# A DeltaNet layer with a multiplicative feed-forward: the second inverse in PSUM, weight signs by a GpSimd product, and another order of steps

## The chip, the cores and the metric

The kernel runs on one core of a Trainium2 chip. A core has five engines with queues of their own, which run in parallel and wait for one another by semaphores: TensorE (PE, matrix products, results in PSUM), VectorE (DVE), ScalarE (ACT), GpSimd (POOL) and SyncE (SP, which here issues most DMA transfers). The metric is the time of one execution on the device in microseconds; lower is better. The profile's span, from the first to the last instruction, is some microseconds shorter than the timed execution.

## The reference

```python
# attention: q, k, v of (B, H, S, D) = (4, 8, 768, 48), beta of (4, 8, 768)
k_n = k / (norm(k, axis=-1) + 1e-6)
for t in range(S):
    y[t] = q[t] @ state
    v_old = k_n[t] @ state
    state = state + beta[t] * outer(k_n[t], v[t] - v_old)
# feed-forward on x = y as (3072 tokens, 384 features)
a = x @ w1                # (384, 1024)
b = x @ w2                # (384, 1024)
h = a * b @ w3            # (1024, 1024)
out = h @ w_out           # (1024, 384)
```

The inputs are single precision, but for the four weight matrices, which come as doubles: each weight is two 32-bit words.

## The kernel before

**Attention.** The 768 tokens are cut into 12 chunks of 64 (index m or c), and two chunks make a unit j or u. Within a chunk the recurrence is a triangular system: the kernel computes the scores of keys with keys and queries with keys (`scores`, step `s`), inverts the unit lower triangular matrix, and applies it. The inverse is done for 32x32 blocks: the blocks of two chunks are written to DRAM and read back so that each of the 128 partitions has one whole block (`to_blocks`, step `u`; tile `Ub`). `inverse` (step `V`) then eliminates in 31 steps on VectorE, each a product into `tb` and a subtraction from the matrix V. Before the change V of unit 0 lies in PSUM (it takes one of the two buffers `ps_w` from `two_banks()` and keeps it, marked in `held`, until it is copied back to `Vb`), and V of the other five units lies in SBUF. The result goes through DRAM once more into `TT`, and `corner` (step `e`: a VectorE transpose L421, two rounds of TensorE products, two pairs of ScalarE copies) makes the 64x64 inverse from its blocks. `chain` (step `c`) carries the state from chunk to chunk, `outputs` (step `y`) makes y and, for the second chunk of a unit, issues the transfers that complete the tile `xT` (L601).

**Feed-forward.** The product w3 w_out is folded into one matrix `w34` of 1024x384: `transpose_w3` (step `t`) turns pieces of w3, `fold` (step `f`, two halves) multiplies them by w_out (`wo`). `wo` lies in the memory of `w2s`, so w2's pieces can be written only where the folds have read it. Then for each unit `ab` (step `a`, eight per unit: product with w1, ScalarE copy, product with w2, VectorE product) and `o` (step `o`, four per unit). These two steps are most of TensorE's work.

**Weights.** `piece` (step `P`) turns doubles into singles in four steps: the transfer into one of five buffers `raw` (shared with the tile `a` of `ab`), two ScalarE activations (absolute value of the high word, scaled; the low word, scaled), a shift left by 3 and an instruction that sets the sign bit from the high word on VectorE (L625, L626), and an integer addition of the low part on GpSimd (L630). P0 to P7 are w_out, P8 to P23 w3 (P of 8 + n belongs to t of n), P24 to P29 w1 and P30 to P35 w2, the first three of each for `a` steps 0 to 3.

**The order.** Each step is a generator; the string ORDER, written out, names the steps one by one, and a name's nth place is its nth stretch up to a `yield`. The program text, and with it the order of instructions in each engine's queue, follows ORDER exactly (`in_text_order`). Letters not told above: `k`, `q`, `v` load, `p` loads the permuted k and q that `d` transposes on VectorE, `K` and `Q` do the same by TensorE for the first two chunks, `g` squares and sums, `N` norms, `n` scales v by norms.

Of the kernel before, what the change touches and what calls it, by code (L numbers as in the profile page):

```python
# [51 lines left out]
v3 a01 a01 a01 a00 a00 a00 P29 P29 a02 P29 P29 a02 c1 a03 a03 a04 k5 g2 d4 V1 e2 g2 g2 c2 n3
n3 e2 e2 e2 a07 d4 d4 P35 P35 e2 e2 d4 e3 e3 P33 a05 n2 n2 c2 g2 s4 N2 e3 s4 s4 s4 P34 P34
c2 P35 P34 e3 e3 s4 P33 P33 P33 a07 a04 s4 a06 c2 y2 p5 d5 d5 u4 c2 P34 y2 P35 a04 p5 d5 d5
c2 a05 a05 a05 v4 n4 s5 s5 s5 c3 c3 a04 a06 a06 a06 V2 s5 s5 u5 s5 e3 c3 a07 k6 c3 y3 V2 a07
o03 o03 V2 V2 V2 y3 V2 V2 V2 V2 V2 V2 V2 V2 V2 o00 V2 p6 p6 g3 y3 n4 V2 V2 V2 V2 V2 o03 V2
V2 V2 v5 V2 V2 V2 V2 V2 V2 o01 o01 o01 o00 o02 a13 a13 o02 a14 a14 V2 V2 V2 V2 V2 e4 e4 g3
a12 a15 a15 o02 d6 d6 a12 a12 a12 a10 a10 e5 e4 c3 a14 e5 e4 c3 n5 c4 e4 e4 c4 a13 a13 a14
e5 k7 g3 g3 g3 V3 c4 a16 a16 c4 c4 c4 y4 y4 d6 v6 d6 g3 g3 a17 s6 g3 N3 s6 s6 s6 s6 s6 n5
a17 a17 p7 d7 d7 p7 d7 o00 d7 a16 c5 c5 e5 k8 e5 e5 a17 a15 s7 s7 a15 s7 s7 s7 s7 u6 u7 a16  # L60
a11 c5 a10 c5 a11 a11 v7 y5 y5 n6 a10 a11 o10 g4 o13 o13 V3 V3 V3 g4 o10 V3 V3 V3 V3 V3 V3
V3 V3 V3 y5 a25 a25 p8 p8 o10 a23 a23 o13 V3 V3 V3 V3 V3 V3 V3 V3 V3 V3 V3 V3 o12 o12 V3 V3
V3 V3 V3 V3 V3 V3 V3 e6 g4 e6 a26 a26 o11 o11 o11 a26 e7 a25 c5 e7 c5 g4 e6 a23 k9 a23 e6
a25 n6 a26 g4 g4 c6 g4 e6 e6 a21 c6 c6 d8 d8 d8 d8 a21 g4 c6 a24 a24 y6 N4 c6 c6 y6 a24 s8
s8 s8 s8 p9 p9 d9 d9 p10 a22 e7 s8 s8 a24 d9 d9 a21 s9 s9 e7 s9 s9 V4 a22 a22 s9 a21 c7 n7
n7 c7 s9 u8 u9 V4 V4 V4 a22 V4 V4 V4 e7 e7 a27 c7 o12 k10 v8 n8 a20 a20 V4 V4 c7 a20 a27 a27
y7 y7 c7 a27 v9 a20 o21 o23 y7 a36 o21 o21 o23 o23 V4 V4 V4 g5 g5 V4 V4 V4 o20 V4 V4 o20 d10
a36 V4 V4 V4 V4 c7 a36 V4 V4 V4 V4 V4 n8 V4 V4 V4 V4 V4 a35 a35 k11 p10 V4 V4 V4 g5 a36 e8
e8 a34 a34 g5 g5 g5 a35 a30 a30 e8 a35 c8 c8 a31 v10 e8 e8 d10 d10 d10 g5 g5 s10 N5 s10 n10
s10 o22 o22 e9 e9 a31 a34 a34 e8 c8 e9 a30 e9 e9 c8 c8 a37 a37 y8 c8 c9 a30 n9 n9 o22 c9 y8  # L70
p11 a37 d11 s10 p11 e9 d11 a33 a33 d11 d11 s10 s10 s11 s11 s11 s11 s11 s11 u10 u11 a32 a32
a37 a31 a31 a32 c9 c9 a32 V5 V5 V5 V5 V5 a33 c9 y9 y9 y9 V5 a33 o20 V5 V5 o33 o33 o33 V5 V5
V5 o31 o31 o31 V5 V5 V5 V5 V5 V5 V5 c9 a43 a43 a43 V5 V5 V5 a43 v11 a40 a40 V5 V5 V5 V5 V5
V5 a47 a47 V5 V5 V5 V5 V5 V5 a42 a42 o32 o30 o30 a44 c10 a44 o32 n11 V5 e10 e10 e10 a42 a42
a41 n11 a41 a47 n10 a47 c10 e10 e10 o32 a40 e10 c10 e11 e11 e11 c10 a40 a44 a44 c10 y10 c10
a41 a41 e11 e11 y10 c11 c11 a46 e11 c11 a45 a45 a45 a45 a46 a46 c11 a46 y11 o30 y11 y11 o40
o40 o40 o42 o42 o42 a53 a53 a53 a53 a50 a52 a50 a52 a51 a51 a51 o41 o41 o43 o43 o43 a51 a50
a50 a55 a55 a55 a55 a56 o41 a56 a56 a56 a57 a52 a52 a57 a57 a57 a54 a54 a54 a54 o51 o51 o51
o50 o50 o50 o52 o52 o53 o53 o53 o52
# [4 lines left out]
def kernel(  # L84
# [286 lines left out]
    def inverse(j):  # L371
        Vb = in_turn(work, [P, BS, BS], "Vb", 1, "Vb")
        pool.memset(Vb[:], 0.0)
        pool.memset(Vb[:].rearrange("p s t -> p (s t)")[:, 0 : BS * BS : BS + 1], 1.0)
# [12 lines left out]
        for s in range(BS - 1):
            n = BS - 1 - s
            t = in_turn(work, [P, 256], "tb", 2, "tb")
            tv = t[:, 0 : (s + 1) * n].rearrange("p (r t) -> p r t", t=n)  # L390
            dve.tensor_tensor(  # L391
                out=tv, in0=V[:, 0 : s + 1, s : s + 1].to_broadcast([P, s + 1, n]),
                in1=U[:, s, s + 1 : BS].unsqueeze(1).to_broadcast([P, s + 1, n]), op=ALU.mult,
            )
# [1 line left out]
            dve.tensor_tensor(out=o, in0=o, in1=tv, op=ALU.subtract)  # L396
# [213 lines left out]
    def piece(n, srcs, dst):  # L610

        raw = in_turn(ffn, [P, CW, 2], "raw", 5, "raw", U32)
        for rows, src in srcs:
# [12 lines left out]
        dve.scalar_tensor_tensor(  # L626
            out=du, in0=hi, scalar=0x80000000, in1=du, op0=ALU.bitwise_and, op1=ALU.bitwise_or
        )
        yield
        pool.tensor_tensor(out=du, in0=du, in1=lo, op=ALU.add)  # L630
# [207 lines left out]
```

## Time and profile before

| | |
|---|---|
| time, median of 3 | 628.66 us (627.59 to 628.71) |
| span of the profiled execution | 623.6 us |
| PE busy | 580.3 us (93%) |
| DVE busy | 352.2 us (56%) |
| ACT busy | 161.1 us (26%) |
| POOL busy | 102.1 us (16%) |
| first product of a step `a` (L694) | at 139.44 us |
| last TensorE instruction ends | at 619.7 us |

Busy shares are means over a kernel of two halves: up to 139 us weights are converted and folded while the first unit goes through attention, and from there on the feed-forward of one unit runs beside the attention of the next. They have to be read by stretches. In a table of groups, the columns are line, engine, operation, output and inputs with their shapes and count, then busy time in us and the mean of one in ns, then the idle time of the engine in front of them and what ended it. In a list by time, the columns are start and length in us, engine, line, operation. Instructions of one engine overlap a little at their ends, so the distance of two starts can be shorter than the first one's length.

### The profile page before, as it was taken

Reading aid. Unit: us, or ns where it says so; the run is one execution under the profiler, and the core shown is the slowest. Engines: PE = TensorE matmul, PEld = TensorE weight load, DVE = VectorE, ACT = ScalarE, POOL = GpSimd, SP = SyncE. Lnnn points to the kernel's source line nnn. Section 1 sums busy time; section 2 is a strip of 40 time slices with the busy share of each in tenths; the row PEclk is TensorE's granted clock in tenths of the full one; section 3 lists DMA queues with packets and bytes.
Section 4 is the critical chain, followed back from the end, with each engine's and each line's share of the span. In section 5 each row is a group of like instructions: output and inputs, shape, how many; then the busy total and the mean of one; then the engine's idle time right before and its main releaser. Section 6 shows DMA issues by size and latency. Waiting matters only on the chain.

```text
span 623.6 us, 17022 instructions
## 1 busy us (share of the span) xinstructions
PE 580.3 (93%) x7372; PEld 343.1 (55%) x7372; DVE 352.2 (56%) x764; ACT 161.1 (26%) x333; POOL 102.1 (16%) x114
## 2 busy tenths in 40 slices
PE   3838779979999999999999999999999999999997
PEld 2724457744575655665556655466564556545454
DVE  3599879999856674667827659464397032100100
ACT  3573236642241112311113111123011022210100
POOL 5364453402321100201002010120001000000000
PEclk9857888999999999999999999999999999999999
DMA  9678966886742724443444453333311200000001
GB/s 207 163 211 169 239 153 140 195 150 107 174 65 52 126 76 87 64 77 80 70 106 52 68 120 73 68 67 43 69 40 39 72 23 3 26 14 25 0 14 38
DMA packets 201835, 55.60 MB, mean 89 GB/s; under 512 B 191969, under 2 KB 195041, under 8 KB 201761
## 3 DMA queue, kind: packets, MB, share of 16 engines
q1 hardware_dynamic: 197600, 53.74, 41.7%
q10 hardware_dynamic: 4160, 0.79, 0.8%
q8 instruction: 58, 0.95, 0.7%
q14 instruction: 17, 0.13, 0.1%
HBM read 42.30 MB, written 11.01 MB: 85 GB/s over the span
## 4 chain that ended last, share of the span: by engine, by line
PE 81%; DMA 7%; SPq 4%; DVE 3%; issue 2%; ACT 2%; POOL 1%; DVEq 0%; ACTq 0%; POOLq 0%
PE ps_f L694 41%; PE ps_f L714 20%; PE ps_w L474 6%; PE ps_w L569 4%; PE ps_w L322 3%; DMA raw<-in_moe_w_dram 3%; SPq L212 2%; PE ps_t L444 2%; PE ps_t L430 2%; PE ps_f L674 2%; DMA vtok<-in_v_dram 1%; DMA ktok<-in_k_dram 1%; DMA X<-in_q_dram 1%; DMA raw<-in_moe_w_out_dram 1%; SPq L614 1%
## 5 line engine op out<-in xcount | busy, mean ns | idle before, releaser
L694 PE MATMUL ps_f<-xT,w1s 128*128 128x512 f32 x288 | 132.9, 605 | 4.3 <-DMA xT<-xT 4.3
L694 PE MATMUL ps_f<-xT,w2s 128*128 128x512 f32 x288 | 131.7, 599 | 0.0
L714 PE MATMUL ps_f<-w,ab 128*128 128x384 f32 x384 | 126.4, 488 | 0.0
L714 PEld LDWEIGHTS ps_f<-w,ab 128*128 128x128 f32 x384 | 72.5, 190 | 51.1 <-issue 3.0
L708 DVE TENSOR_TENSOR ab<-a,ps_f 128x512 f32<-128x512 f32 x48 | 32.5, 683 | 112.7 <-PE ps_f L694 112.6
L694 PEld LDWEIGHTS ps_f<-xT,w1s 128*128 128x128 f32 x288 | 53.9, 192 | 66.0 <-issue 63.2
L694 PEld LDWEIGHTS ps_f<-xT,w2s 128*128 128x128 f32 x288 | 53.1, 190 | 60.3 <-issue 56.8
L703 ACT COPY a<-ps_f 128x512 f32<-128x512 f32 x48 | 27.5, 586 | 142.6 <-PE ps_f L694 132.9
L391 DVE TENSOR_TENSOR tb<-Vb,Ub 128x31 f32<-128x31 f32 (+15 forms) x155 | 55.5, 358 | 13.0 <-DMA Ub<-Ud 8.2
L396 DVE TENSOR_TENSOR Vb<-Vb,tb 128x31 f32<-128x31 f32 (+15 forms) x155 | 58.4, 377 | 5.3
L674 PE MATMUL ps_f<-w2s,w3T 128*128 128x384 f32 x128 | 50.0, 550 | 3.6 <-POOL w2s L630 2.1
L234 POOL TENSOR_TENSOR sq<-ktok 128x384 f32<-128x384 f32 x24 | 20.7, 862 | 152.0 <-DVE ss L236 91.6
L590 ACT COPY xT<-ps_w 48x256 f32<-48x256 f32 x96 | 30.4, 365 | 54.2 <-PE ps_w L569 53.7
L720 ACT COPY osb<-ps_f 128x384 f32<-128x384 f32 x24 | 11.3, 479 | 127.4 <-PE ps_f L714 109.1
L460 POOL TENSOR_TENSOR vtok<-vtok,n 128x384 f32<-128x384 f32 x24 | 19.9, 842 | 130.6 <-DMA vtok<-in_v_dram 104.3
L674 PEld LDWEIGHTS ps_f<-w2s,w3T 128*128 128x128 f32 x128 | 26.8, 215 | 23.3 <-issue 6.9
L322 PE MATMUL ps_w<-KQ 48*64 48x128 f32 x768 | 30.5, 303 | 5.3 <-DVE KQ L285 2.7
L322 PEld LDWEIGHTS ps_w<-KQ 48*64 48x64 f32 x768 | 25.0, 150 | 13.9 <-issue 5.5
L665 PE MATMUL ps_f<-ident,w 128*128 128x128 f32 x64 | 13.4, 363 | 13.5 <-POOL w L630 13.5
L630 POOL TENSOR_TENSOR w<-w,raw 128x512 uint32<-128x512 uint32 x16 | 21.2, 1332 | 26.6 <-ACT w L622 7.8
L534 DVE TENSOR_TENSOR S<-S,ps_w 48x768 f32<-48x768 f32 x20 | 19.0, 949 | 11.0 <-PE ps_w L474 10.7
L331 DVE TENSOR_TENSOR U<-ps_w,wt 128x512 f32<-128x512 f32 x24 | 16.4, 686 | 15.0 <-PE ps_w L322 14.6
(83 smaller groups left out, 558.3 us busy)
## 6 DMA issues: line engine op xcount, KB each, us to landing
raw<-in_moe_w_dram SPq DMA_DIRECT2D x16, 512.0 KB, 6.2
vtok<-in_v_dram SPq DMA_DIRECT2D x24, 192.0 KB, 4.0
raw<-in_moe_w_dram SPq DMA_DIRECT2D x24, 192.0 KB, 4.0
out_dram<-osb SPq DMA_DIRECT2D x24, 192.0 KB, 2.0
ktok<-in_k_dram SPq DMA_DIRECT2D x22, 192.0 KB, 4.3
raw<-in_moe_w_out_dram SPq DMA_DIRECT2D x8, 384.0 KB, 3.8
Ud<-U SPq DMA_DIRECT2D x48, 64.0 KB, 2.0
Ub<-Ud SPq DMA_DIRECT2D x6, 512.0 KB, 4.6
```

The costliest lines, as they stand in the source:

```text
L322: pe.matmul(ps[half(z), h % 2, 128 * (h // 2) : 128 * (h // 2) + 128], lhsT=x[:, 0, :], rhs=x.rearrange("p j t -> p (j t)"), start=True, s ...
L391: dve.tensor_tensor(out=tv, in0=V[:, 0 : s + 1, s : s + 1].to_broadcast([P, s + 1, n]), in1=U[:, s, s + 1 : BS].unsqueeze(1).to_broadcast( ...
L396: dve.tensor_tensor(out=o, in0=o, in1=tv, op=ALU.subtract)
L474: pe.matmul(out(ps, r, h, z), lhsT=lhs(r, h, z), rhs=rhs(r, h, z), start=True, stop=True,)
L569: i = pe.matmul(region(h, z, r), lhsT=lhs, rhs=rhs, start=part[n] not in part[:n], stop=part[n] not in part[n + 1 :],)
L590: act.copy(out=xT[f, p:NP:2, b : b + NR, cc, :].rearrange("p a r t -> p r a t"), in_=pyv[f, z, b : b + NR],)
L630: pool.tensor_tensor(out=du, in0=du, in1=lo, op=ALU.add)
L674: pe.matmul(ps[:, 0:DM], lhsT=w3Ts[jc, kc // 4][:, kc % 4 * P : kc % 4 * P + P], rhs=wo[:, kc], start=(kc == 0), stop=(kc == KF - 1),)
L694: pe.matmul(ps[:], lhsT=w[:, m, js], rhs=x[:, m].rearrange("p b c t -> p (b c t)"), start=(m == 0), stop=(m == KM - 1),)
L703: act.copy(out=a[:], in_=ps[:])
L708: dve.tensor_tensor(out=t[:], in0=a[:], in1=ps[:], op=ALU.mult)
L714: pe.matmul(ps[:, 0:DM], lhsT=abs_[u, jc][:, b * P : (b + 1) * P], rhs=w34[:, jc, :], start=(jc == 0), stop=(jc == KF - 1),)
```

## The change

Three things are changed.

- `inverse` keeps V in PSUM for units 0 and 1 instead of unit 0 alone. For unit 1 this adds two ScalarE copies in front and two behind, and holds one `ps_w` buffer in between.
- `piece` no longer sets the sign bit on VectorE. ScalarE turns the high word into +1 or -1 (Sign, in place, a third activation), and GpSimd multiplies the absolute value by it, after its integer addition. This is to take work from VectorE.
- ORDER is a new one, with the same steps but for the four copies of V1. At its start V0's memset and P11's load come first, and q0's load stands behind P11's activations in ScalarE's queue. The first `a` stands at place 367 in both.

Of the orders only the part up to the first `a` is shown here, beside the rest of the diff.

```diff
-P3 P6 k0 g0 q0 P3 P3 P3 g0 g0 k1 K0 K0 P6 P6 K0 K0 K0 Q0 Q0 Q0 Q0 Q0 g0 g0 g0 g0 K1 K1 K1 K1
-K1 g0 beta beta beta N0 P15 s0 s0 s0 q1 s0 s0 s0 s0 Q1 Q1 Q1 Q1 Q1 P6 P15 P15 P15 s1 s1 s1
-P11 s1 s1 P11 s1 P11 P13 P13 p2 d2 P11 t3 d2 V0 P14 P14 P14 P10 P10 P13 u0 u1 P12 P0 P10 V0
-V0 s1 V0 P12 P12 P0 P0 V0 P13 P14 V0 P10 V0 V0 V0 P2 P2 P2 t5 P12 t5 V0 V0 P0 t4 t3 P1 P1 P1
-V0 V0 V0 P1 t4 t7 t7 P2 P5 P5 P5 t2 P4 V0 t6 t6 P7 f3 P7 P7 P7 p3 k2 t2 f1 V0 V0 P22 P23 f2
-P4 P4 V0 p2 V0 P22 P22 V0 P23 P23 P4 P5 f1 f3 f2 g1 f3 s0 V0 V0 V0 V0 V0 V0 V0 V0 P21 P8 P8
-V0 V0 V0 V0 V0 f2 P23 t15 t15 v0 n0 f1 P22 P9 t14 n0 t14 f7 V0 k3 V0 P16 V0 V0 f7 P17 g1 f7
-P8 g1 g1 P9 P9 V0 d2 P8 t0 P21 d2 s2 P21 g1 g1 P9 e0 t1 P16 P16 t0 P21 t13 e0 e0 g1 t1 g1 N1
-s2 s2 e1 s2 P16 t8 v1 n1 s2 s2 e0 e0 e0 s1 f0 e1 c0 P26 t8 P26 t13 e1 n1 d3 P17 P20 P20 P19
-P19 P17 P17 f0 e1 c0 y0 y0 c0 P26 P20 f0 e1 P19 P20 t12 p3 d3 t12 d3 d3 c0 s3 s3 t9 s3 s3
-P26 P27 P27 s3 P19 t11 s3 c1 c1 u2 P28 P28 P28 e1 f6 P27 k4 V1 g2 g2 c1 P18 P18 P18 t11 c1
-P28 P24 P24 t9 P24 u3 P25 f6 y1 V1 V1 V1 V1 P27 P25 P25 V1 V1 f6 V1 c1 V1 V1 y1 V1 V1 V1 V1
-P18 t10 t10 g2 p4 V1 V1 V1 V1 V1 f4 V1 P31 f5 P31 P30 P30 P30 V1 f4 v2 P32 f4 f5 P32 P32 y1
-P24 P25 a02 P31 a02 V1 V1 V1 V1 V1 V1 V1 p4 V1 V1 f5 a03 g2 V1 V1 V1 a03 P30 P32 a00 P31 a01
...
+V0 P11 k0 g0 k1 g0 g0 P11 P11 P1 P11 q0 K0 K0 K0 K0 K0 P3 K1 g0 g0 P1 P1 P1 K1 K1 K1 K1 g0
+g0 P3 P3 Q0 P14 Q0 Q0 Q0 P3 Q0 beta beta t3 g0 P14 beta q1 Q1 Q1 Q1 N0 p2 Q1 Q1 s0 P14 P14
+s0 s0 s0 s0 s0 s0 P0 P0 s1 s1 s1 s1 s1 P12 P12 s1 P0 P0 P12 P12 P15 P15 P15 P15 P13 P13 P13
+P13 u0 u1 P10 V0 V0 t3 P10 d2 d2 V0 P10 V0 V0 V0 V0 V0 V0 P10 v0 n0 P2 P2 P2 P2 t4 t4 t7 V0
+V0 V0 P6 P6 P6 P6 V0 V0 t7 t5 t5 P5 P5 P5 P5 t2 t2 V0 V0 P4 P4 P4 V0 V0 s1 p2 P7 P7 P4 P22
+P7 P7 V0 V0 t6 t6 f2 s0 P22 P22 V0 V0 p3 V0 V0 V0 P9 P9 P9 P23 P23 P16 P22 f1 f1 f2 V0 V0
+P23 f1 V0 f2 n0 t14 t14 P21 P21 P8 P8 V0 V0 P9 V0 V0 V0 V0 P23 k2 g1 g1 f3 f3 V0 V0 k3 g1 P8
+P8 g1 g1 P21 t15 P16 P16 t15 f3 P18 P18 f7 f7 V0 f7 d2 d2 s2 P16 t8 P17 P17 t0 t1 d3 d3 t8
+g1 g1 e0 e1 e0 e0 t1 g1 N1 P18 s2 s2 t0 e0 s2 s2 P19 s2 P21 t13 t13 P17 e0 v1 f0 e0 c0 V1
+P18 t10 P19 c0 y0 y0 e1 e1 e1 p3 d3 d3 P17 s3 t9 s3 s3 P25 s3 s1 s3 s3 P20 P20 P19 P19 c0
+P25 P20 f0 f0 P25 P24 n1 n1 P26 e1 P24 e1 u2 u3 V1 V1 V1 P27 t10 p4 t9 P20 c0 c1 f4 c1 c1
+P27 V1 P24 V1 V1 V1 V1 V1 t12 t12 f4 f4 f6 P24 V1 V1 v3 c1 V1 P26 y1 y1 P25 P27 P27 t11 t11
+P30 V1 V1 V1 P26 V1 P26 k4 g2 P31 v2 n2 f5 P30 f6 f6 V1 V1 V1 V1 P30 V1 c1 f5 f5 P30 V1 V1
+V1 P31 P31 y1 a03 a02 V1 V1 P31 P32 P32 P32 P32 a02 V1 V1 V1 V1 V1 V1 V1 V1 a03 k5 P29 P29
+P29 P29 g2 d4 d4 a00 a02 a03 p4 a00 a00 V1 V1 P28 P28 V1 a02 a01 g2 g2 g2 c1 c2 P28 g2 n2
...
@@ -377,7 +377,7 @@
         sync.dma_start(out=U[:], in_=Uds.pop(j)[:])
         yield
         V = Vb
-        if j == 0:
+        if j < 2:
 
             V = two_banks().rearrange("p a (s t) -> p (a s) t", t=BS)
             held.add(("w", turns["w"]))
@@ -395,7 +395,7 @@
             o = V[:, 0 : s + 1, s + 1 : BS]
             dve.tensor_tensor(out=o, in0=o, in1=tv, op=ALU.subtract)
             yield
-        if j == 0:
+        if j < 2:
             for i in range(0, BS, BS // 2):
                 act.copy(out=Vb[:, i : i + BS // 2], in_=V[:, i : i + BS // 2])
                 yield
@@ -621,13 +621,12 @@
 
         act.activation(out=dst, in_=hi.bitcast(FP32), func=ACTF.Abs, scale=2.0**-112)
         act.activation(out=lo, in_=lo, func=ACTF.Copy, scale=2.0**-29)
+        act.activation(out=hi.bitcast(FP32), in_=hi.bitcast(FP32), func=ACTF.Sign)
         yield
         dve.tensor_scalar(out=du, in0=du, scalar1=3, scalar2=None, op0=ALU.logical_shift_left)
-        dve.scalar_tensor_tensor(
-            out=du, in0=hi, scalar=0x80000000, in1=du, op0=ALU.bitwise_and, op1=ALU.bitwise_or
-        )
         yield
         pool.tensor_tensor(out=du, in0=du, in1=lo, op=ALU.add)
+        pool.tensor_tensor(out=dst, in0=dst, in1=hi.bitcast(FP32), op=ALU.mult)
         yield
 
     w1s = const.tile([P, KM, DF], FP32, name="w1s")
```

More of the change, by code (lines that the diff above doesn't have):

```diff
@@ L50 @@
-P18 t10 t10 g2 p4 V1 V1 V1 V1 V1 f4 V1 P31 f5 P31 P30 P30 P30 V1 f4 v2 P32 f4 f5 P32 P32 y1
-P24 P25 a02 P31 a02 V1 V1 V1 V1 V1 V1 V1 p4 V1 V1 f5 a03 g2 V1 V1 V1 a03 P30 P32 a00 P31 a01
[L52 to L79, printed above, removed]
+V0 P11 k0 g0 k1 g0 g0 P11 P11 P1 P11 q0 K0 K0 K0 K0 K0 P3 K1 g0 g0 P1 P1 P1 K1 K1 K1 K1 g0
@@ new lines @@
+V1 P31 P31 y1 a03 a02 V1 V1 P31 P32 P32 P32 P32 a02 V1 V1 V1 V1 V1 V1 V1 V1 a03 k5 P29 P29
+P29 P29 g2 d4 d4 a00 a02 a03 p4 a00 a00 V1 V1 P28 P28 V1 a02 a01 g2 g2 g2 c1 c2 P28 g2 n2
+a03 e2 e2 e2 g2 P33 e2 P33 a00 d4 d4 a01 a01 e3 P34 P34 c2 e2 e2 g2 N2 s4 s4 s4 P34 a01 P28
+a04 s4 n3 s4 c2 P33 P33 s4 a05 a05 c2 c2 P35 P35 p5 P35 P35 P34 y2 a07 e3 e3 c2 p5 y2 a04 d5
+d5 p6 d5 d5 u4 s5 s5 s5 s5 s5 a06 e3 e3 c3 n3 c3 s5 a06 u5 V2 V2 V2 V2 V2 V2 V2 a06 a06 e3
+c3 V2 a07 a07 a05 a04 c3 y3 y3 y3 a07 a05 a04 o02 o02 o01 V2 V2 V2 V2 V2 V2 V2 V2 o02 V2 V2
@@ new lines @@
+V2 a15 a15 a15 V2 o01 V2 V2 V2 a14 v4 n4 V2 V2 V2 V2 V2 V2 V2 V2 V2 V2 V2 o03 o03 a15 d6 d6
+o00 V3 e4 e5 e4 c3 c3 e4 o01 a14 o00 a14 a14 k6 g3 g3 g3 e4 e4 e5 e4 c4 n4 c4 a12 a12 e5 e5
+g3 p7 k7 c4 v5 c4 o00 p6 d6 d6 g3 e5 a12 c4 a17 y4 y4 a12 n5 c4 c5 n5 v6 c5 a17 g3 g3 g3 N3
+a13 d7 d7 o03 a10 a10 a10 p7 a10 d7 d7 a13 s6 s6 s6 k8 p8 e5 s6 s6 u6 s6 a17 a17 s7 s7 s7 s7
+s7 a11 a11 g4 u7 s7 a11 a11 V3 V3 V3 p8 a13 a13 c5 c5 g4 a16 a16 a16 v7 V3 c5 a16 o12 o12 c5
+c6 o12 y5 y5 y5 o10 o10 o10 o11 o11 V3 V3 V3 n7 V3 V3 V3 V3 V3 a27 a27 a27 n6 n6 V3 c6 V3 V3
@@ new lines @@
+V3 V3 V3 V3 V3 V3 V3 a21 V3 V3 d8 d8 d8 o11 d8 a27 V3 V3 V3 V3 V3 V3 V3 V3 V3 k9 e6 s8 a21
+a25 o13 o13 e6 a26 o13 a25 a26 a26 e6 g4 g4 g4 g4 g4 a24 g4 N4 s8 s8 e7 e7 s8 e6 e6 e6 s8 s8
+a21 a21 a26 e7 c6 c6 a24 a24 a24 p9 p9 c6 c6 y6 y6 d9 a23 d9 d9 p10 d9 a20 s9 a20 s9 s9 a23
+s9 s9 n7 a25 a25 c7 c7 k10 g5 V4 u8 u9 V4 s9 e7 e7 g5 V4 V4 V4 V4 V4 a22 e7 c7 c7 V4 V4 V4
+V4 a22 a22 g5 a23 a20 a20 a22 V4 y7 y7 c7 a23 o22 o22 d10 d10 p11 o23 V4 o23 V4 V4 V4 y7 a36
+V4 V4 V4 V4 V4 c7 g5 a32 a32 v8 V4 V4 V4 V4 V4 a35 a36 a35 V4 V4 V4 V4 V4 V4 V4 p10 a31 a31
@@ new lines @@
+a32 o21 a32 V4 e8 n8 e8 o22 e9 e9 n8 o23 c8 e8 e8 k11 a37 a37 e8 o20 e8 c8 c8 c8 o21 a33 a33
+a33 d10 d10 c8 c8 a33 g5 o20 o20 y8 g5 y8 g5 a35 a35 a30 e9 e9 g5 N5 v9 n9 c9 n9 c9 a36 a36
+s10 e9 s10 s10 s10 p11 s10 e9 a34 a34 v10 d11 d11 d11 d11 c9 c9 a30 s10 a34 s11 o21 s11 s11
+s11 s11 s11 a37 a37 a34 u10 a31 a31 a30 a30 V5 u11 V5 V5 V5 y9 y9 y9 V5 V5 V5 V5 V5 V5 V5 c9
+o31 o31 o30 a41 o30 o30 o31 V5 V5 V5 V5 V5 V5 V5 V5 V5 V5 n10 a44 a44 a41 a42 a42 a45 a45
+a41 V5 V5 V5 V5 a44 v11 V5 V5 V5 V5 V5 V5 V5 V5 n10 o33 V5 a41 c9 o32 o32 e10 e10 e10 o33
@@ L80 @@
+o33 o32 c10 a44 e11 a42 a42 e10 e11 e10 a46 e10 c10 c10 c10 e11 a46 a46 n11 a46 c10 a47 c10
+a40 a40 a40 a47 a47 a47 c11 n11 c11 e11 e11 e11 a43 a40 a43 a43 a43 y10 y10 c11 a45 c11 y11
+a45 o41 o43 y11 y11 o41 o41 o43 o43 a54 a56 a56 a54 a54 a53 a53 a54 a53 a53 o42 o42 a52 o40
+o40 o40 a50 a52 a56 a50 a50 a56 a50 a55 a55 a55 a55 a57 a57 a57 a57 a51 a52 a52 a51 a51 o42
+a51 o50 o50 o50 o51 o51 o51 o53 o53 o53 o52 o52 o52
 """
```

## The prediction

> **What bounds the kernel now.** I first cut the execution into stretches and read the busy columns of each (TensorE, weight loads, VectorE, ScalarE, GpSimd, then the granted clock).
>
> ```profile
> core 0: us, PE busy (x) PEld busy (x) DVE busy (x) ACT busy (x) POOL busy (x), PEclk, DMA share, GB/s
> 0.00:31.00 31.00, 18.07 (x396) 15.90 (x396) 13.11 (x34) 13.54 (x24) 13.57 (x23) 0.93 0.88 186
> 31.00:51.00 20.00, 6.67 (x26) 5.00 (x26) 18.89 (x36) 13.68 (x28) 10.98 (x10) 0.59 0.76 199
> 51.00:89.30 38.30, 31.05 (x114) 18.31 (x114) 31.08 (x71) 13.76 (x26) 17.80 (x18) 0.83 0.80 186
> 89.30:139.40 50.10, 45.32 (x948) 32.17 (x948) 46.04 (x90) 27.63 (x57) 18.64 (x17) 0.93 0.82 168
> 139.40:619.70 480.30, 479.18 (x5888) 271.72 (x5888) 243.06 (x538) 92.00 (x201) 41.07 (x49) 1.00 0.32 62
> ```
>
> From 139.4 us on TensorE never pauses (479.2 of 480.3 us), and its work is untouched. All that can change is when this starts. Ahead of it TensorE idles 38 us and runs partly at a granted clock of 0.59 to 0.93, VectorE is full (18.9 of 20 us, later 46 of 50), and GpSimd and ScalarE are half idle. So the question is the first `a` product, which stands at place 367 of either order, behind the same folds, scores and chains.
>
> Next the chain that ended last. It goes through weight pieces on VectorE at 38 to 44 us, then, at the end of the first stretch, through this:
>
> ```profile
> 135.39 0.59 SPq L601
> ...
> 136.71 2.60 DMA xT<-xT
> 139.44 25.04 PE ps_f L694 x54
> ```
>
> The folds were done at 135.1; TensorE waited 4.3 us for the transfer of xT, which stood on SyncE behind weights.
>
> Last the instructions in order of time, VectorE beside GpSimd.
>
> ```profile
> 50.69 0.37 DVE L391 TENSOR_TENSOR tb<-ps_w,Ub 128x207 f32<-128x207 f32 x1
> 51.09 0.38 DVE L396 TENSOR_TENSOR ps_w<-ps_w,tb 128x207 f32<-128x207 f32 x1
> ...
> 141.40 0.41 DVE L391 TENSOR_TENSOR tb<-Vb,Ub 128x247 f32<-128x247 f32 x1
> 141.84 1.41 DVE L396 TENSOR_TENSOR Vb<-Vb,tb 128x247 f32<-128x247 f32 x1
> ```
>
> ```profile
> 50.12 1.98 POOL L630 TENSOR_TENSOR w2s<-w2s,raw 128x384 uint32<-128x384 uint32 x2 [4.76 <-issue]
> ...
> 141.70 1.28 POOL L630 TENSOR_TENSOR w2s<-w2s,raw 128x512 uint32<-128x512 uint32 x1 [13.21 <-DMA qperm<-in_q_dram]
> ```
>
> With the inverse's matrix in PSUM (50 us) a step runs at its own length under a GpSimd addition; with it in SBUF (142 us) 0.42 us become 1.41.
>
> **What the Trainium skill says.** "SBUF — State Buffer", Who interferes with whom: a VectorE instruction with two SBUF inputs, or a `tensor_scalar` in a 2-port mode, and a GpSimd instruction that reads SBUF exclude one another for a whole instruction; at most one SBUF input outside these modes does not contend. The four lines above agree; the shift (L625) can contend, and stretches from 0.42 to 1.45. "GPSIMD Engine Reference", Engine selection: two-input elementwise work is about half as fast there as on VectorE; here 1.28 against 0.69 us at 512 columns. "ScalarE: Activation LUTs", Table sets: cheap functions are in every set, a switch costs about 2.7 us. Sign isn't listed there by name; the trace has one load of 1.28 us. I take none added, at worst one.
>
> **The change, part by part.**
>
> Signs. 36 pieces: 8 of 384 columns, 28 of 512. Off VectorE goes L626:
>
> ```profile
> L626 DVE SCALAR_TENSOR_TENSOR w<-raw,w 128x512 uint32<-128x512 uint32 x16 | 15.5, 967 | 0.6
> L626 DVE SCALAR_TENSOR_TENSOR w2s<-raw,w2s 128x384 uint32<-128x384 uint32 x8 | 5.9, 743 | 0.3
> L234 POOL TENSOR_TENSOR sq<-ktok 128x384 f32<-128x384 f32 x24 | 20.7, 862 | 152.0 <-DVE ss L236 91.6 <-DMA ktok<-in_k_dram 60.5
> L345 POOL TENSOR_TENSOR PT<-PT,smask 128x512 f32<-128x512 f32 x4 | 5.5, 1382 | 8.3 <-ACT PT L343 8.3
> ```
>
> with its other two rows (5.6 and 5.1) 32.1 us in all, some 27 of them for the 30 pieces ahead of the first `a`. ScalarE gains a Sign per piece at the pace of the Copy beside it (starts 0.57 us apart at 512 columns, 0.45 at 384): 22 x 0.57 + 8 x 0.45 = 16 us ahead of the first `a`. GpSimd gains a float product per piece: 0.83 at 384 (undisturbed L234); at 512 between 1.1 (0.83 by width) and 1.38 (L345), I take 1.25: 22 x 1.25 + 8 x 0.83 = 34 us. My sums of all work queued ahead of the first `a` go from 98 to 81 us on VectorE, 71 to 87 on ScalarE, 54 to 83 on GpSimd. The fullest engine has 87 instead of 98, and no long VectorE instruction but the shift can be held by GpSimd's longer stay.
>
> The new wait: a piece's `raw` (five in turn, shared with `a`) is released after the product, 1.25 us later. Behind it on SyncE wait all later transfers.
>
> V1 in PSUM. Two copies in and two out on ScalarE: 4 x 0.59 = 2.4 us, hidden. VectorE's steps keep their length (0.42 to 0.43 at 255 columns in both forms) and lose the stretches, about 1 us for each addition that hits. It takes one of the two `ps_w` for the whole inverse. Its users in that time are c1's three products and y1: each needs the one before it evicted, or needs its result, so I cost this at nothing. c1's last subtotal waits for y1's copies, but only c2 needs it.
>
> New order, followed through. (1) V0's first step comes at 44.1 now: after chunk 1's last U (31.5) VectorE worked through six pieces, 12.6 us with stretches. Now five shifts and two transposes stand there, about 4 us; the step waits for `Ub` (issued 34.9, 5.4 to landing: 40.3) and for ScalarE's copies into PSUM behind five pieces (31.5 plus about 9). So 41: 3 us won. (2) V0 takes 30.1 us now, 4.7 of it L626 of seven pieces. New: eight shifts, one more (0.45), and GpSimd busy about 19 of 27 us instead of 13 of 30; I add 1 us of holds. 26.8; done at 67.8 instead of 74.3. (3) Now 14.3 us pass until the corner's transpose (L421, 88.6), 4 of them because VectorE still has pieces and q transposes when TT is there (84.7). New: copies 1.2, Vd 5.0, four TT issues and landing 4.3: 78.4, and VectorE is free by then. TensorE is not quite, with fold 7 and half of chunk 2's scores in front: corner at 81 instead of 89.4. (4) From there TensorE is the limit: now 45.7 us without a pause to the last fold. New: the products between e0 and the first `a`, by the pieces of the chain (eight half folds of 2.85, two TTR of 2.0, corners 4 x 1.13, and so on), add up to 44.5 us. c0's X has N1, two shifts and four score evictions before it, and comes at 90.7 where TensorE would want it at 89: 2 us. Done at 127.5 to 128. (5) xT: y1's products are followed by 10 us of folds on TensorE; copies 2.6, issues 3.75 and landing 2.6 take 9, so the 4.3 us go.
>
> First `a` at 128 instead of 139.4: 11.4 us won. After it P31 and P32 leave GpSimd at about 130; three w1 products (8.3 us) cover this. P28 leaves it by 140 and is wanted at 153. 628.7 - 11.4 = **617.3 us**.
>
> **The rivals.**
> - *GpSimd becomes the bound*. 83 us of queued work, most of it after 24 us, plus a hold of 0.3 for each of 30 shifts, leaves hardly 10 us of slack to 128. If half of the pieces wait 1.2 us more for a slot (15 x 1.2 = 18, half absorbed), 9 us are lost: 626. For it: GpSimd waits on ACT and DVE for each piece; against: half its time is idle now. 0.15.
> - *Everything overlaps*: the idle between 31 and 139 us (26 us) falls to 8 and half the time lost at low clock (about 11 us: busy time by one minus the clock, 31 to 100 us) comes back: 23 less, 606. For it: the queues are even; against: the early chain k, q, scores, V0 can't be shortened. 0.12.
> - *Slower*: ScalarE in order holds evictions behind pieces whose data isn't there. P21 and P8 stand before V0's copies out, P27 and P26 before y1's, the first piece before q0's load. 5.7 us is the longest such wait now; three on the chain are 17 against the 11.4 won: 634. Against it: DMA isn't full (0.76 to 0.82 of its time). 0.18.
>
> **How the numbers follow.** Forecast 0.55, the three rivals 0.15, 0.12, 0.18. The unknown costs (product 1.1 to 1.38, table 0 to 2.7, holds 0 to 8) move the forecast from 613 to 623. From 607 to 629 leaves out the end of the fast rival and most of the slower one. Faster: 0.78 (the first three, but for the edge of the GpSimd case), same 0.04, slower 0.18.
>
> **What would show it.** The first product with `w1s` at about 128 us with no wait for xT in front; L421 first at about 79; V0's steps within 27 us; no V1 step over 0.6 us; GpSimd's rows on weights at some 87 us in all (45 now and 42 of products); VectorE busy below 90% from 89 us on. Wrong if SyncE's waits for GpSimd's product (18 us for L630 now) double and ScalarE waits for `raw` more than today's 26 us, or if TensorE pauses after its start, waiting for weights.

## The result, and the profile after

The changed kernel takes **619.47 us** (median of 4 runs, 616.58 to 621.14) against 628.22 us before (4 runs beside it, 627.59 to 628.71): ratio **0.9856, 95% interval 0.9814 to 0.9899**. On a second chip the same kernel gave 0.9879 (0.9835 to 0.9924). The profiled run of the changed kernel spans 616.5 us, that of the kernel before 623.6. The latter's time, 625.40 us, is some 3 us below its median, so the profiles show less of a gain (7.1 us) than the medians (8.75 us).

First the stretches of the changed kernel, with the columns as in the prediction (TensorE, weight loads, VectorE, ScalarE, GpSimd, granted clock) and cut at its own first corner product (77.7) and first `a` product (128.88):

```profile
core 0: us, PE busy (x) PEld busy (x) DVE busy (x) ACT busy (x) POOL busy (x), PEclk, DMA share, GB/s
0.00:31.00 31.00, 16.57 (x400) 14.49 (x400) 14.31 (x34) 19.76 (x35) 22.13 (x31) 1.00 0.96 202
31.00:51.00 20.00, 9.84 (x30) 6.36 (x31) 15.29 (x35) 14.06 (x29) 18.67 (x17) 0.57 0.88 209
51.00:77.70 26.70, 23.69 (x107) 13.56 (x105) 23.74 (x55) 19.54 (x37) 24.29 (x23) 0.94 0.96 238
77.70:128.88 51.18, 44.68 (x950) 31.27 (x950) 35.86 (x83) 28.31 (x58) 29.17 (x26) 0.97 0.77 154
128.88:612.60 483.72, 479.34 (x5888) 271.14 (x5887) 232.08 (x523) 99.97 (x215) 51.52 (x57) 1.00 0.32 64
```

VectorE is no longer the full engine of the fourth stretch (70% busy; 46.04 of 50.1 us before), GpSimd has become one of the full ones of the second and third, and the products from the first `a` on begin 10.56 us earlier (128.88 for 139.44). But what follows has grown. The last line stops at 612.60, 0.5 us before TensorE's last product ends (613.14): from the first `a` product to that end it takes 484.3 us, where it took 480.3 for the same work. So 4.0 us are given back behind the start.

TensorE in order of time shows both sides. The bracket is its idle time ahead of the line and what ended it.

```profile
77.71 1.20 PE L430 MATMUL ps_t<-T,U 32*32 32x32 f32 x64
...
94.85 0.84 PE L474 MATMUL ps_w<-X,ktok 64*48 64x48 f32 x55 [2.04 <-issue]
...
112.83 4.27 PE L673 MATMUL ps_f<-w2s,w3T 128*128 128x384 f32 x8 [4.15 <-ACT w3T L667]
...
126.19 2.85 PE L673 MATMUL ps_f<-w2s,w3T 128*128 128x384 f32 x8
128.88 7.89 PE L693 MATMUL ps_f<-xT,w1s 128*128 128x512 f32 x18
...
150.37 1.20 PE L430 MATMUL ps_t<-T,U 32*32 32x32 f32 x64 [2.23 <-DVE T L421]
151.50 4.54 PE L693 MATMUL ps_f<-xT,w2s 128*128 128x512 f32 x6
```

The wait for `xT` (4.3 us before) is gone: the first `a` product follows its fold at once. In its place stand 4.15 us in front of a fold whose transposed weights come late, and after the start 2.23 us in front of the second inverse's corner product.

ScalarE shows where the 4.15 us come from:

```profile
110.52 0.68 ACT L622 ACTIVATE w1s<-raw 128x512 f32<-128x512 f32 x1 [6.51 <-DMA raw<-in_moe_w_dram]
111.11 0.65 ACT L623 ACTIVATE raw<-raw 128x512 uint32<-128x512 uint32 x1
111.66 0.65 ACT L624 ACTIVATE raw<-raw 128x512 f32<-128x512 f32 x1
112.20 0.57 ACT L667 COPY w3T<-ps_f 128x512 f32<-128x512 f32 x1
```

ScalarE stood 6.51 us before piece P27, whose load SyncE had issued only at 103.76, behind the load of V1's `Ub` that was itself waiting for `Ud`. The copy of `w3T`, whose transposes had ended at 106.10, stood behind P27 until 112.20. The third operation here, L624, is the new Sign.

VectorE beside GpSimd, as in the prediction, first VectorE:

```profile
115.74 0.41 DVE L391 TENSOR_TENSOR tb<-ps_w,Ub 128x240 f32<-128x240 f32 x1
116.19 0.42 DVE L396 TENSOR_TENSOR ps_w<-ps_w,tb 128x240 f32<-128x240 f32 x1
116.51 0.67 DVE L626 TENSOR_SCALAR w1s<-w1s 128x512 uint32<-128x512 uint32 x1
...
117.99 0.42 DVE L391 TENSOR_TENSOR tb<-ps_w,Ub 128x252 f32<-128x252 f32 x1
```

and GpSimd at the same time:

```profile
115.61 1.28 POOL L629 TENSOR_TENSOR w1s<-w1s,raw 128x512 f32<-128x512 f32 x1
117.31 1.29 POOL L628 TENSOR_TENSOR w1s<-w1s,raw 128x512 uint32<-128x512 uint32 x1 [0.42 <-DMA raw<-in_moe_w_dram]
```

No step of V1 is held under either GpSimd operation any more (0.41 to 0.42 us; one of 1.41 us was shown before). Only the shift is (L626 here; 0.67 us, 0.42 alone). GpSimd's product (L629) takes 1.28 us at 512 columns, like its addition.

### The profile page after: what moved, and what is told of

It reads as the page before. It is cut to its first block, busy times and chain, and to the rows that moved or that the text cites. A ratio compares the mean times of both kernels' runs of the same rounds, so it can differ in the third digit from the quotient of the medians.

```text
span 616.5 us, 17062 instructions
## 1 busy us (share of the span) xinstructions
PE 574.7 (93%) x7372; PEld 336.8 (55%) x7372; DVE 321.3 (52%) x728; ACT 182.1 (30%) x373; POOL 145.8 (24%) x150
## 4 chain that ended last, share of the span: by engine, by line
PE 74%; DMA 11%; SPq 6%; DVE 4%; issue 2%; ACT 1%; POOL 0%; DVEq 0%; ACTq 0%
PE ps_f L693 36%; PE ps_f L713 20%; PE ps_w L474 5%; DMA raw<-in_moe_w_dram 4%; PE ps_w L569 4%; SPq L212 3%; PE ps_w L322 3%; SPq L365 2%; PE ps_f L673 2%; PE ps_t L430 2%; PE ps_t L444 2%; DMA X<-in_q_dram 2%; DMA Ub<-Ud 2%; DMA Ud<-U 1%; DMA Vd<-Vb 1%
## 5 line engine op out<-in xcount | busy, mean ns | idle before, releaser
L693 PE MATMUL ps_f<-xT,w1s 128*128 128x512 f32 x288 | 131.4, 599 | 0.0
L693 PEld LDWEIGHTS ps_f<-xT,w1s 128*128 128x128 f32 x288 | 53.1, 190 | 59.5 <-issue 56.3
L673 PE MATMUL ps_f<-w2s,w3T 128*128 128x384 f32 x128 | 48.6, 532 | 6.6 <-ACT w3T L667 4.2
L391 DVE TENSOR_TENSOR tb<-Vb,Ub 128x31 f32<-128x31 f32 (+15 forms) x124 | 44.2, 356 | 19.1 <-DMA Ub<-Ud 15.3
L719 ACT COPY osb<-ps_f 128x384 f32<-128x384 f32 x24 | 11.4, 480 | 118.4 <-PE ps_f L713 97.8
L396 DVE TENSOR_TENSOR Vb<-Vb,tb 128x31 f32<-128x31 f32 (+15 forms) x124 | 43.5, 351 | 4.3
L673 PEld LDWEIGHTS ps_f<-w2s,w3T 128*128 128x128 f32 x128 | 25.3, 205 | 24.8 <-ACT w3T L667 4.8
L322 PE MATMUL ps_w<-KQ 48*64 48x128 f32 x768 | 26.6, 284 | 0.3 <-ACT PT L343 0.3
L322 PEld LDWEIGHTS ps_w<-KQ 48*64 48x64 f32 x768 | 22.4, 140 | 7.8 <-issue 6.1
L391 DVE TENSOR_TENSOR tb<-ps_w,Ub 128x31 f32<-128x31 f32 (+15 forms) x62 | 21.0, 339 | 8.6 <-DMA Ub<-Ud 7.0
L664 PE MATMUL ps_f<-ident,w 128*128 128x128 f32 x64 | 12.7, 339 | 13.4 <-POOL w L629 10.8
L516 DVE TENSOR_TENSOR X<-ps_w,wt 128x384 f32<-128x384 f32 x24 | 12.2, 552 | 24.5 <-PE ps_w L474 24.5
```

What stands on the lines that cost most here:

```text
L322: pe.matmul(ps[half(z), h % 2, 128 * (h // 2) : 128 * (h // 2) + 128], lhsT=x[:, 0, :], rhs=x.rearrange("p j t -> p (j t)"), start=True, s ...
L391: dve.tensor_tensor(out=tv, in0=V[:, 0 : s + 1, s : s + 1].to_broadcast([P, s + 1, n]), in1=U[:, s, s + 1 : BS].unsqueeze(1).to_broadcast( ...
L673: pe.matmul(ps[:, 0:DM], lhsT=w3Ts[jc, kc // 4][:, kc % 4 * P : kc % 4 * P + P], rhs=wo[:, kc], start=(kc == 0), stop=(kc == KF - 1),)
L693: pe.matmul(ps[:], lhsT=w[:, m, js], rhs=x[:, m].rearrange("p b c t -> p (b c t)"), start=(m == 0), stop=(m == KM - 1),)
```

## The experiments

All ratios are to the kernel before on the same chip. "L421" is the first corner transpose, after V0; the next columns are how long it then takes to the first `a` product, and from there to TensorE's last instruction, in the one profiled run of each (us).

| kernel | ratio (95%) | L421 | to first `a` | to the end |
|---|---|---|---|---|
| before | 1 | 88.60 | 50.8 | 480.3 |
| order only | 0.9970 (0.9949-0.9990) | 80.52 | 51.4 | 486.7 |
| signs only | 1.0136 (1.0100-1.0173) | 91.97 | 55.3 | 485.3 |
| V1 in PSUM only | 1.0071 (1.0048-1.0094) | 88.16 | 54.9 | 484.1 |
| order and V1, old signs | 0.9911 (0.9876-0.9946) | 79.72 | 49.5 | 492.2 |
| order and signs, V1 in SBUF | 0.9929 (0.9909-0.9948) | 75.59 | 53.3 | 490.6 |
| all three (the change) | 0.9856 (0.9814-0.9899) | 75.78 | 53.1 | 484.3 |
| the change again, second chip | 0.9879 (0.9835-0.9924) | 80.76 | 55.1 | 484.4 |
| the change without the product | 0.9852 (0.9826-0.9879) | 77.40 | 51.9 | 486.5 |
| signs only, without the product | 0.9912 (0.9880-0.9943) | 84.00 | 55.8 | 480.4 |
| P27 early | 0.9872 (0.9843-0.9902) | 75.85 | 55.6 | 484.2 |
| P27 and V1 early | 0.9898 (0.9866-0.9930) | 74.86 | 54.1 | 484.4 |
| and xT ahead | 0.9916 (0.9882-0.9950) | 76.55 | 49.7 | 491.1 |

A caution for all readings of one profile: the two profiled runs of the change itself have L421 at 75.78 and 80.76. In the second the transfers of the stretch from 31 to 51 us filled 0.75 of the DMA engines' time, in the first 0.88, and what follows came 5 to 7 us later (the first `a` product at 135.88 instead of 128.88). Their second and third lengths agree to 2 us. So absolute places are read to some 7 us, lengths and ends of waits more closely, and the verdicts go by the ratios.

**Each part alone.** *Order only* is the changed kernel with the old signs and V1 in SBUF (V1's four copies are dropped from the order).

```diff
-        if j < 2:
+        if j == 0:
...
-        act.activation(out=hi.bitcast(FP32), in_=hi.bitcast(FP32), func=ACTF.Sign)
...
+        dve.scalar_tensor_tensor(
+            out=du, in0=hi, scalar=0x80000000, in1=du, op0=ALU.bitwise_and, op1=ALU.bitwise_or
+        )
...
-        pool.tensor_tensor(out=dst, in0=dst, in1=hi.bitcast(FP32), op=ALU.mult)
```

> The new order alone: signs set on VectorE as before, V of unit 1 in SBUF (the four steps of its copies taken out of the order). My theory, that the order pays because VectorE's queue became shorter: 30 sign instructions, some 20 us, are back in front of the first product of step a, so V0 takes about 30 us again and the corner, c0 and N1 come later; first product at 135 to 140 us, time 624 to 629. Rival, that the order does it all: first product at 129 us, time 619 to 620.

626.5 us, a time as expected, but not for the reason given: the start moved by 7.5 us, to 131.94, earlier than the 135 to 140 of my theory, and most of it was returned: the stretch behind the start is 6.4 us longer, 5.9 of them in four pauses of 1.40 to 1.55 us (for w2s, twice for `ab`, once for the second inverse's transpose).

*Signs only* is the kernel before, old order and V1 in SBUF, with the new signs.

```diff
+        act.activation(out=hi.bitcast(FP32), in_=hi.bitcast(FP32), func=ACTF.Sign)
...
-        dve.scalar_tensor_tensor(
-            out=du, in0=hi, scalar=0x80000000, in1=du, op0=ALU.bitwise_and, op1=ALU.bitwise_or
-        )
...
+        pool.tensor_tensor(out=dst, in0=dst, in1=hi.bitcast(FP32), op=ALU.mult)
```

> The old order with the new signs (Sign on ScalarE, product on GpSimd), V of unit 1 in SBUF. My theory: VectorE is relieved, V0 ends about 4 us earlier and the corner with it, but the wait for xT behind weights on SyncE and the order of the folds stay: first product at 133 to 136 us, time 622 to 626. Rival, that the order does it all: no change, 628, or slower, 630 and more, because each buffer of raw words is kept 1.3 us longer and GpSimd's additions hold VectorE's steps on V1 in SBUF twice as often.

638.11 us: my expectation was wrong, the rival's right; the first `a` product came at 147.29. TensorE's transposes of pieces wait for GpSimd's product, 24.4 us in all beside 13.5 for its addition before:

```profile
35.24 1.11 PE L664 MATMUL ps_f<-ident,w 128*128 128x128 f32 x4 [4.67 <-POOL w L629]
39.63 1.11 PE L664 MATMUL ps_f<-ident,w 128*128 128x128 f32 x4 [3.28 <-POOL w L629]
47.75 3.68 PE L664 MATMUL ps_f<-ident,w 128*128 128x128 f32 x16 [7.01 <-POOL w L629]
...
76.97 1.11 PE L664 MATMUL ps_f<-ident,w 128*128 128x128 f32 x4 [7.90 <-POOL w L629]
```

*V1 in PSUM only*: old order, old signs; the two copies in stand right after V1's `Ub`, the two out after its last step.

```diff
-        if j == 0:
+        if j < 2:
```

> The old order and the old signs, V of unit 1 in PSUM (its two copies in after the load of Ub, its two copies out after its last step). My theory: V1's steps lose their stretches of 1 us, some 6 us in all, but none of them stands in front of the first product, and TensorE does not wait for V1 later: 627 to 629, the same. Rival, that the inverse in PSUM is a main part of the gain: 624 or less.

632.55 us: wrong again. Two new pauses of TensorE carry it:

```profile
128.49 1.53 PE L474 MATMUL ps_w<-X,ktok 64*48 64x48 f32 x64 [3.18 <-ACT xT L590]
...
157.11 8.37 PE L694 MATMUL ps_f<-xT,w2s 128*128 128x512 f32 x15 [3.62 <-ACT a L703]
```

and ScalarE in front of the second:

```profile
155.40 1.07 ACT L400 COPY Vb<-ps_w 128x512 f32<-128x512 f32 x2 [8.57 <-DVE ps_w L396]
```

The first is the `ps_w` that V1 holds: c1's subtotal waits for y1's copies out of the only one left. The second is ScalarE's queue: V1's copies out stood there 8.57 us until the last step was done, with a copy of `a` behind them. This second pause is a matter of where I put the copies, and another place was not tried.

**Two parts of three.** The old signs in the changed kernel, and V1 back in SBUF in it; their edits are those above.

> The changed kernel with the signs set on VectorE as before: new order and V of unit 1 in PSUM. My theory: as the order alone but without stretches on V1, first product at 134 to 139 us, time 623 to 628. Rival, that order and PSUM do it: 619 to 620.

621.92 us: faster than I expected, near the rival, and the first `a` product came at 129.18, as early as in the change. Its profiled run (626.57 us, a span of 624.8) is slower than its median, so its last length is not leaned on.

> New order and new signs, with the second inverse's V left in SBUF (its two copies in and its two copies out are left out of the order). Theory (the edits pay together: with GpSimd doing two passes of 1.3 us for every 512 columns of weights, VectorE's steps on V in SBUF are held while those in PSUM are not): V1's 62 operations, 0.42-0.43 us each at the wide middle in the changed kernel, stand at up to 1.4 us when a GpSimd operation lies beside them, some 8 to 12 us more busy time on VectorE between 100 and 150 us; the L421 transpose of V1 comes later than 149.6 us and the TensorE pause before it (2.23 us in the changed kernel) grows: 622 to 627 us. Rival (V1 has slack, so PSUM for it is worth nothing): 618 to 621 us.

623.83 us, as the theory had it. The start is where the change has it (128.86), and all is lost behind it. V1 begins at 106.84 and ends at 147.23, 40.4 us, against 106.89 to 139.48 with PSUM; 16 of its operations are held, some 15 us in all, such as these:

```profile
123.41 1.40 DVE L396 TENSOR_TENSOR Vb<-Vb,tb 128x247 f32<-128x247 f32 x1
124.85 1.39 DVE L391 TENSOR_TENSOR tb<-Vb,Ub 128x252 f32<-128x252 f32 x1
```

V1 is only 7.8 us longer for it, since with PSUM it stands waiting 6.5 us for ScalarE in between (behind shifts of P30 to P32). The corner transpose comes at 155.15 instead of 149.60, and TensorE pauses for w2s (1.80, 2.62), for the transpose (1.12) and for `ab` (1.63). The stretch after the start is 490.6 us long; V1 in PSUM brings it to 484.3 (484.4 in the second profile of the change).

**Does GpSimd's product cost anything?** It is left out, in the new order and in the old.

```diff
-        pool.tensor_tensor(out=dst, in0=dst, in1=hi.bitcast(FP32), op=ALU.mult)
```

> The changed kernel without GpSimd's product by the sign: that product is left out, so the weights come out as absolute values. GpSimd loses some 44 us of its 146 us busy. Theory (GpSimd is not on the path; its product only holds VectorE's shifts a little and keeps a raw buffer some 1.3 us longer): 617 to 619.5 us, first product of the first token part at 127 to 129 us. Rival (GpSimd's doubled work is what eats the missing part of the gain): 614 or less, first product by 125 us.

618.87 us, no different from the change, and the first `a` product at 129.34, behind a wait of 1.85 us for `xT`: in the new order 44.7 us of GpSimd work cost nothing that can be measured. VectorE's eight shifts within V0 fall from 6.52 to 3.66 us, but V0 still takes 27.9 us (28.3), since VectorE now waits 1.80 and 0.52 us for ScalarE there.

> The old order with the new signs, V1 in SBUF, but without GpSimd's product by the sign: that product is left out, so the weights come out as absolute values. ScalarE's third operation, the sign, stays. Theory (in the old order the new signs cost 8.6 us because GpSimd, 18.6 of 20 us busy between 31 and 51 us, keeps each of the five raw buffers longer and so holds SyncE's next loads and TensorE's transposes): with the product gone, GpSimd is back near 11 us busy in that stretch, the first product of the first token part comes at 137 to 140 us, and the time is 623 to 628 us. Rival (it is ScalarE's third operation, or the place of VectorE's shift, that costs): 633 to 638 us.

623.12 us, where signs only took 638.11 (ratios 0.9912 and 1.0136): in the old order the product costs some 2.2%, 14 us. Without it the new signs gain 0.9% there: VectorE's relief is worth something by itself, and the product takes it and more. The stretches 31 to 78 us of both, first with the product:

```profile
31.00:51.00 20.00, 5.48 (x23) 4.68 (x24) 15.59 (x32) 16.06 (x32) 18.56 (x17) 1.00 0.63 173
51.00:78.00 27.00, 17.88 (x58) 10.19 (x57) 19.48 (x49) 11.38 (x23) 18.11 (x18) 0.90 0.86 185
```

and without:

```profile
31.00:51.00 20.00, 9.53 (x29) 6.28 (x30) 13.87 (x40) 19.70 (x41) 12.16 (x12) 0.50 0.86 221
51.00:78.00 27.00, 22.34 (x66) 12.95 (x65) 14.77 (x41) 8.55 (x16) 11.18 (x11) 0.86 0.83 203
```

With the product GpSimd is full (18.56 of 20 us), the transfers fill 0.63 of their time instead of 0.86, and TensorE does 4 us less in either stretch. SyncE shows one way in which it holds the rest back:

```profile
SPq L614 <- POOL w L629: 21.0, 8, 4.4
SPq L614 <- POOL w2s L629: 10.6, 4, 5.5
```

Twelve times, 31.6 us in all (us in total, times, longest), the next load of a piece waited for GpSimd to release a `raw`; before, and without the product, such waits were 18.0 and 11.5 us. The other way is direct: TensorE's transposes wait 12.2 us for GpSimd without the product and 24.4 with it. How the 14 us divide between the two was not separated. Both belong to my GpSimd rival, which so holds in the old order. In the changed kernel the waits of the loads for the product add up to 10.7 us, those of the transposes to 10.8.

**Is the 4.15 us pause worth removing?** P27 is loaded ahead of V1's `Ub`, and ScalarE takes it after the `w3T` copy.

```diff
-u2 u3 V1 V1 V1 P27 t10 p4
+u2 u3 P27 V1 V1 V1 t10 p4
...
-c1 c1 P27 V1 P24 V1 V1 V1 V1 t12 t12 f4
+c1 c1 V1 P24 V1 V1 V1 V1 t12 t12 P27 f4
```

> The changed kernel with one transfer and one step moved: the raw load of P27 is issued ahead of the load of V1's U, which waits for a transfer (so it is issued near 100 us instead of 103.76), and ScalarE takes P27 after the copy of w3T for t12 instead of ahead of it. Theory (ScalarE stood 6.51 us before P27 with the w3T copy behind it, and TensorE paused 4.15 us for that copy): the pause at 112.83 us goes or is under 1.5 us, the half fold after it takes 2.85 instead of 4.27 us, the first product of the first token part comes 3 to 5 us earlier, near 124 to 126 us; part of it is given back at the second inverse's corner product, which is late by itself and then waits 4 to 6 us instead of 2.23: 617 to 619.5 us. Rival (the copy is late for another reason, or xT of c1 takes the wait's place at once): the first product stays at 128 to 129 us and the time at 619 to 620.

620.37 us, the first `a` product at 131.43. The pause for `w3T` is gone, and another wait took its place at once, as the rival said, though for c1's X and not for `xT`:

```profile
117.29 1.11 PE L569 MATMUL ps_w<-KQ,S 48*48 48x64 f32 x32 [5.44 <-DVE X L516]
```

The load of `Ub` went out 1.4 us later (104.76) and, beside P27's now, took 6.1 us to land instead of 3.5. V1 began at 110.94 instead of 106.89, and c1's X stands behind eight of its steps in VectorE's queue (116.13 instead of 112.08).

Next, besides, `Ud` goes out ahead of P26, c1's X stands ahead of V1's first step, ScalarE takes P31 ahead of f5's copy, and VectorE's shifts of P30, P31 and P32 stand a few steps of V1 later.

```diff
-P26 e1 P24 e1 u2 u3 P27 V1 V1 V1
+e1 P24 e1 u2 u3 P26 P27 V1 V1 V1
...
-c1 f4 c1 c1 V1 P24 V1
+c1 f4 c1 c1 c1 V1 P24 V1
...
```

> As the run before it, and V1 started and finished earlier too: the loads of U for V1 go to DRAM ahead of P26's raw load, c1's X goes ahead of V1's first step on VectorE, ScalarE takes P31 ahead of the f5 copy, and VectorE's shifts of P30, P31 and P32 stand behind a few more of V1's steps. Theory (both pauses come from steps that wait at the head of a queue): V1's first step at 103 to 106 us instead of 106.89, its last by 133 to 136 us instead of 139.3, the pause of 2.23 us before the corner product is gone or the product comes 3 to 5 us earlier, and the time is 613 to 616.5 us. Rival (the end is set by the products after the first token part and by weights, so that an earlier second inverse brings nothing): 617 to 620 us.

621.46 us: the theory fell. `Ub` was issued earlier (101.58), but V1 began at 109.51, now behind c1's X, which waited 5.65 us for its product. That product stood on TensorE behind a half fold that took 4.76 us (the granted clock was 0.56 from 99.9 to 106.5). V1 ended at 140.03, and the pause before its corner product was 1.26 us. The folds were done at 126 us, and TensorE waited 3.00 us for `xT`, whose issues stood on SyncE behind P31's load.

> The run with P27 and V1 earlier, and one step more: the transfers of xT for the first token part are issued ahead of P31's raw load, which waits for a raw buffer, instead of behind it and a load of v. There the products had been ready at 126 us and waited 3.00 us for xT. Theory (that wait was all that stood between the earlier products and the end): xT is issued near 119.5 us, the first product comes at 126 to 126.5 us without a wait, and the time is 1.5 to 3 us below the changed kernel beside it. Rival (the weights P31 and P32, and the second inverse behind them, come no earlier, so that the products wait there instead): the first product at 126 us too, new pauses of 2 to 3 us between 130 and 155 us, and the same time as the changed kernel within 1 us.

```diff
-k4 g2 P31 v2
+k4 g2 y1 P31 v2
...
-V1 P31 y1 a03
+V1 P31 a03
```

624.54 us beside 621.34 for the change (ratios 0.9916 and 0.9879, the intervals overlap): no gain. The first `a` product did come at 126.24, without a wait:

```profile
126.24 5.31 PE L693 MATMUL ps_f<-xT,w1s 128*128 128x512 f32 x12
132.55 2.84 PE L693 MATMUL ps_f<-xT,w1s 128*128 128x512 f32 x6 [0.99 <-ACT w L680]
138.27 1.10 PE L693 MATMUL ps_f<-xT,w2s 128*128 128x512 f32 x2 [2.87 <-ACT a L702]
139.98 2.08 PE L693 MATMUL ps_f<-xT,w2s 128*128 128x512 f32 x2 [0.62 <-POOL w2s L629]
```

ScalarE stood 6.37 us before P31 and 2.90 before P32, whose loads came after `xT`, with f5's copy and `a`'s behind them. Of the rival's two statements the pauses came, and the time was not within 1 us but, if anything, longer.

> The changed kernel itself, once more, on the same chip as the two runs beside it, so that these are compared with it there. All theories: ratio 0.984 to 0.989, 618 to 621 us; the first product of the first token part within 1 us of 128.9 us if nothing in it is left to chance.

621.34 us, ratio as expected; the first product came at 135.88, not within 1 us of 128.9: it *is* left to chance. The two profiles part early: V0's first step already came at 42.74 instead of 39.00. The transfers of the first 50 us are the likely cause; this was not tested.

## Why the prediction was right, and where not

The time (617.3 forecast, 619.47 measured) was near, and the gain came from an earlier start, as the mechanism had it. That the start fell at 128.88, beside 128 forecast, is in part luck: step 3 was 3.3 us too late and step 4 4.7 us too short, and the second profile has it at 135.88. The steps, by the first profile:

1. **V0's first step, 41**: 39.00, with 1.97 us of waiting for `Ub` in front, the transfer I named.
2. **V0 in 26.8 us with 1 us of holds**: 28.3. Its eight shifts took 6.52 us. Alone they are five of 0.35 and three of 0.42, 3.0 us: the holds are 3.5 us, not 1. The run without the product shows that this is not time won back by itself: the holds went, waits for ScalarE came.
3. **Corner transpose at 78.4, corner products at 81**: 75.78 and 77.71. `Vd` landed in 3.6 us and not in the 5.0 I carried over, and TensorE had the fold and the scores that I had put in front behind it by then: 3.3 us too late.
4. **44.5 us of products and 2 us of waiting from there**: 44.68 us busy, 1.4 of them by the slowed half fold at 112.83, so the sum of the products was right to about 1 us; the idle time was 6.5 us (4.15 for `w3T`, 2.04 inside c0's last products, the rest in small gaps), and the total 51.2. I had looked for waits at c0's X only. This is the mechanism of my *slower* rival (ScalarE in its order holds a copy behind a piece that has not landed), and I had named P27, though in front of y1's copies; on this chain it struck once and not three times. The Trainium skill, "PSUM — Partial Sum Buffer", Engine vs sequencer instructions, states that the queues of ScalarE, VectorE and GpSimd are strict FIFO; this case agrees: ScalarE stood 6.51 us for a load with which the copy of 0.57 us behind it has nothing to do.
5. **The 4.3 us for `xT` go**: yes.
6. **Behind the start, weights are covered**: here the step failed. I checked P31, P32 and P28, and TensorE waited no more than 0.5 us for weights; I did not check V1's own chain. V1's first step waited 5.08 us for `Ub`; its later steps stand on VectorE behind shifts of P30, P31 and P32, which waited for ScalarE (1.86, 2.76 and 1.92 us). So the corner product came 2.23 us late, the six products behind it took 4.54 us instead of 2.84, and 0.91 us were lost at 191.5. These are 4.8 us, and some 0.8 us come back in small amounts elsewhere, which leaves the 4.0 us given back: 10.56 won, 6.6 kept at TensorE's end in the profiled runs. By the medians 8.75 us were kept (7.9 on the second chip), of 11.4 forecast.
7. **V1 in PSUM at nothing**: right with the order, wrong without. Holding a `ps_w` and placing the copies cost 4 us in the old order (ratio 1.0071). With the new one, the PSUM edit is the step from 0.9929 to 0.9856 (second chip 0.9879): 3 to 5 us. The intervals lie apart for the first and overlap a little for the second; the stretch behind the start is 6 us shorter in both profiles of the change. I had counted the stretches that V1 loses, and no time for them.
8. **Signs**: the sizes were right: GpSimd's rows on weights add up to 89.2 us (87 forecast), no second table load came (one, 1.28 us), VectorE lost 31 us. But I argued, beside the chain, from the sum of the fullest queue (87 instead of 98 us), as if the load set the start. These sums do not follow from their parts: 98 less 27 is 71 on VectorE, not 81, and 54 plus 34 is 88 on GpSimd, not 83, and what else the orders place differently is not said there. Up to the first `a` product VectorE was busy 89 us (109 before), ScalarE 82 (69) and GpSimd 94 (61), so the fullest was GpSimd, and 617.3 did not rest on the sums. The runs leave it open what the signs are worth: with the other two parts in place the new signs take 0.9911 to 0.9856 (second chip 0.9879), intervals that overlap; by themselves they cost 1.4%. A sum of work says nothing of who releases what. SyncE's waits for GpSimd, which I had named as a sign of being wrong if they doubled from 18 us, fell to 10.7.

So what made the gain? Not any one edit: two of them lose time by themselves, the order gains 0.3%, and the three together 1.2 to 1.4%. In single profiles the order brings L421 some 8 us forward and the signs with the order 4 more, which is within the spread of such places (the second profile of the change has it where the order alone does); V1 in PSUM keeps what is won there from being lost behind the start. The GpSimd rival was a true mechanism, which the order avoids. The old order with the signs and V1 in PSUM together was not run, how much of the order's part comes from which of its moves was not tried, and no order was found that removes the pauses left in the changed kernel and is faster.

## What to carry to other kernels

In a kernel whose order is written out by hand, price an edit together with the order: ask what each engine's queue holds behind the instruction that becomes later, and which buffer it releases, before adding up busy time. A pause of a few us that ends with one engine's copy need not be worth its length, since another queue may be only a few us behind: three orders that removed pauses here gained nothing. And follow the second chain of the same kind (here V1) as closely as the first, through to the point where it is consumed.
